# Loading weight blocks from ScalarE's DMA queue, each behind an exponential, in a fused attention and feed-forward kernel

## The chip, the cores and the metric

The kernel runs on one core of one Trainium2 chip. The metric is the device time of one execution in microseconds. Engines are named as in the profile: PE is TensorE (matmuls; PEld its weight loads), DVE is VectorE, ACT is ScalarE, POOL is GpSimd, and SP is SyncE, which issues DMAs. A row "SPq" is SP's DMA queue.

## The reference

Masked attention over 8 batches of 8 heads with 576 rows and a head size of 64, and behind it a feed-forward layer of 512 to 2048 to 512 with softplus on all 4608 tokens:

```python
scores = scale * np.matmul(q, k.transpose(0, 1, 3, 2))
thresh = np.max(scores, axis=-1, keepdims=True) - tau
scores = np.where(scores >= thresh, scores, -1000000000.0)
scores = scores - np.max(scores, axis=-1, keepdims=True)
attn = np.exp(scores)
attn = attn / (np.sum(attn, axis=-1, keepdims=True) + 1e-09)
attn_out = np.matmul(attn, v).astype(np.float32)
x = attn_out.transpose(0, 2, 1, 3).reshape(B * S, H * D)
h = x @ w_in
g = np.maximum(h, 0.0) + np.log1p(np.exp(-np.abs(h)))
return (g @ w_out).astype(np.float32)
```

q, k, v and tau are float32. The weights w_in (512 x 2048) and w_out (2048 x 512) arrive as 64-bit floats, so the kernel has to make 32-bit ones of them.

## The kernel before

**Attention.** The work is 32 units, a batch and a pair of heads each, and each unit has 9 query tiles of 128 rows: 288 tiles. A tile goes through a fixed chain: scores on PE (L423, tile `s`), the row maximum and the threshold on DVE (`negm`, `thr`, L430 and L431), the exponential on ACT (`exps`, L435, into one half of `e_all`), the mask by threshold and the row sum on DVE (`mask`, L440, in place in `e_all`), the transpose of the weights on PE (L471, L474, tiles `tm` and `tr`), and a copy of them by ACT (`gH`, L498 to L519). `e_all` and `s` have two halves, so two tiles are in flight at a time. ACT also casts the transposed keys (`kT`, L368 and L390) and queries (`qT`, `qm`, L377 and L396) for PE.

**Feed-forward.** The 4608 tokens are 9 chunks of 512. Their matmuls (`h` L645 to L649, `o` L703 to L707) are mixed between the attention tiles, from the moment the weights are there.

**Weights.** They come in 32 blocks of 512 KB. i0_0 to i3_3 are blocks of w_in (128 rows by 512 columns), o0 to o15 of w_out; about one new block starts every two tiles. The function `to_f32` takes one block through these steps:

- a DMA of the 64-bit words into `words` (the profile's `wc_i` or `wc_o`; L185),
- `first`, set down `WD = 4` points (two tiles) later: ACT's Abs of the high words, scaled, into `wa_i` or `wa_o` (L193), and POOL's clamp (L194),
- `second`, three steps on DVE (L200, L202, L205), each put behind the latest emitted mask by an order dependency (`behind`, with the list `masked`),
- `parts`, two steps on POOL that split the block into a high and a low part (L125, L132),
- for w_in, two stores on SP to a scratch tensor in HBM (`wi_d`, L234), from which the feed-forward stage loads it again.

All DMAs are on SP's queue: the words of the weights, the loads of k, q and v (`kn`, `qn`, `vn`, L306 to L321), the swaps of halves of the queries (L385, L386), the stores of the weights' parts and of the attention's output (`x_d`, L597), the feed-forward's loads. SP executes them in order, so a load stands behind whatever waits ahead of it.

`took` is the number of weight-sized buffers that a block finds free for its words and its scratch. It is 2 for 29 of the 32 blocks; for o12, o14 and o15 it is less.

**What sets the order.** The program emits the instructions in a planned sequence, and a scheduler of the framework then orders each engine's instructions by its own model of durations, within the dependencies. `tc.add_manual_dep(..., NoSync, ...)`, called by `behind`, adds a dependency that holds on the same engine's order without a semaphore. A semaphore that tells that a DMA has landed is one of eight, taken in turn over all DMAs; a DMA waits until the one that used its semaphore before has landed.

Of the kernel before, what the change touches and what calls it, by code (L numbers as in the profile page):

```python
# [11 lines left out]
U32 = mybir.dt.uint32  # L12
AF = mybir.ActivationFunctionType
# [46 lines left out]
def tile_kernel(ctx: ExitStack, tc: tile.TileContext, q, k, v, tau, w_in, w_out, out):  # L60
# [8 lines left out]
    nc = tc.nc  # L69
# [5 lines left out]
    HS = S // 2  # L75
# [47 lines left out]
    def hi_of(eng, out_, in_):  # L123
        if eng is nc.gpsimd:
            eng.tensor_scalar(out=out_, in0=in_, scalar1=1.0, scalar2=1.0, op0=ALU.mult, op1=ALU.mult)  # L125
        elif eng is nc.scalar:
            eng.copy(out_, in_)  # L127
        else:
            eng.tensor_copy(out_, in_)  # L129

    def lo_of(eng, out_, in_, hi):
        eng.tensor_tensor(out=out_, in0=in_, in1=hi.bitcast(F32), op=ALU.subtract)  # L132
# [3 lines left out]
    free, held = [NFC], [0]  # L136

    masked = []
    scored = []

    def behind(i, others):

        if others:
            tc.add_manual_dep(i.ins, others[-1].ins.name, mybir.DependencyInfo(
                mybir.DependencyClass.NoSync, mybir.DependencyReason.DATA), reason="order")

    def piece(dt, name):
        return cpool.tile([P, 2, DM], dt, tag="wo", bufs=NFC, name=name)

    def to_f32(src, want, name, then):  # L150

        keep = 1 if want else 0
        while free[0] < 1 + keep and free[0] < NFC - held[0]:
            force()
        took = max(0, min(2, free[0] - keep))
        if took:
            words = piece(F32R, f"wc_{name}")
        else:  # L160
            words = wpool.tile([P, 2, DM], F32R, tag="wi", bufs=WB, name=f"wc_{name}")
        if took > 1:
            m = piece(F32, f"wa_{name}")[:, 0, :]
        else:
            m = fpool.tile([P, 512], F32, tag="st", bufs=NST, name=f"ws_{name}")
        free[0] -= took + keep
        held[0] += keep

        later_ = defer if took > 1 else lambda n, f: f()
        step = 2 if held[0] < NFC // 2 else 1  # L170
        w = piece(F32R, f"wo_{name}") if want else words

        def done():
            free[0] += took

        def parts():
            hi_of(nc.gpsimd, w[:, 0, :], m)
            lo_of(nc.gpsimd, w[:, 1, :], m, w[:, 0, :])

        if src.dtype == F32:  # L180
            nc.sync.dma_start(m, src)
            later_(WD, lambda: then(parts, w, done))
            return
        words = words.bitcast(U32).rearrange("p a n -> p (a n)")
        nc.sync.dma_start(words, src.bitcast(U32))  # L185
        words = words.rearrange("p (n t) -> p n t", t=2)
        low, high = words[:, :, 0], words[:, :, 1]
        mu = m.bitcast(U32)

        def first():
            nc.scalar.activation(m, high.bitcast(F32), AF.Abs, scale=2.0 ** 16)  # L193
            nc.gpsimd.tensor_scalar(out=m, in0=m, scalar1=W_MAX, scalar2=W_MIN, op0=ALU.min, op1=ALU.max)  # L194
            later_(1, lambda: second(0))


        def second(n):
            if n == 0:
                i = nc.vector.tensor_scalar(out=mu, in0=mu, scalar1=3, scalar2=None, op0=ALU.logical_shift_left)  # L200
            elif n == 1:
                i = nc.vector.scalar_tensor_tensor(out=mu, in0=high, scalar=0x80000000, in1=mu,  # L202
                                                   op0=ALU.bitwise_and, op1=ALU.bitwise_or)
            else:
                i = nc.vector.scalar_tensor_tensor(out=mu, in0=low, scalar=29, in1=mu,  # L205
                                                   op0=ALU.logical_shift_right, op1=ALU.bitwise_or)
            if took > 1:
                behind(i, masked)
            if n < 2:
                later_(step, lambda: second(n + 1))  # L210
            else:
                later_(1, lambda: then(parts, w, done))

        later_(WD, first)
# [12 lines left out]
    def prep_w_in(g, cc):  # L227
        def split(parts, w, free):
            parts()
            defer(WS, lambda: store(w.bitcast(F32), free))  # L230

        def store(w, free):
            for i in range(2):
                nc.sync.dma_start(wi_d[g][:, :, i, cc, :].rearrange("f p e -> p f e"),  # L234
                                  w[:, i, :].rearrange("p (f e) -> p f e", f=4))
            free()
            if cc == NCC - 1:
                ready.add(("i", g))

        to_f32(w_in[cc * P:(cc + 1) * P, g * 512:(g + 1) * 512], False, f"i{g}_{cc}", split)  # L240

    def prep_w_out(fc):
        def split(parts, w, free):
            wo[fc] = w
            parts()
            free()
            ready.add(("o", fc))

        to_f32(w_out[fc * P:(fc + 1) * P, :], True, f"o{fc}", split)
# [25 lines left out]
    for b in range(B):  # L275
        for kind in (("one", "two") if b < NSPLIT else ("all",)):
            for hp in range(NPAIR):
                s = Unit()
# [123 lines left out]
    e_all = cpool.tile([P, 2, S], F32, name="e_all")  # L402
# [29 lines left out]
        s.m[t] = (negm, thr)  # L432

    def exps(s, t):
        nc.scalar.activation(e_all[:, s.half[t], :].rearrange("p (h n) -> p h n", h=2), s.sp[t][:, :, 0:HS],  # L435
                             AF.Exp, bias=s.m[t][0], scale=1.0)

    def mask(s, t):
        e2 = e_all[:, s.half[t], :].rearrange("p (h n) -> p h n", h=2)
# [362 lines left out]
    def force():  # L802
        _, f = later.pop(0)
        f()
# [32 lines left out]
    for kind, g in WL:  # L837
        for m in range(4):
            n = len(prep)
# [75 lines left out]
    scores(*tiles[0])  # L915
    row_max(*tiles[0])
    exps(*tiles[0])
    scores(*tiles[1])
    for j in range(2):
# [4 lines left out]
    for g, (cur, t) in enumerate(tiles):  # L924
# [5 lines left out]
        for step in PAT0 + ("m" if g == TG - 1 else "") if g < TG else PAT:  # L930
            if step == "T":
                weights_T(cur, t)
            elif step == "h":
                weights_hi(cur, t)
            elif step == "l":
                weights_lo(cur, t)
            elif step == "R" and nxt:
                row_max(*nxt)
            elif step == "e" and nxt:
                exps(*nxt)  # L940
            elif step == "m" and nxt:
                mask(*nxt)
            elif step == "M":
                mask(cur, t)
            elif step == "f":
                upto += quota / PAT.count("f")
                while done < upto:
                    done += next(ffn)
            elif step == "x":
                extras(cur.i, cur.tiles.index(t))  # L950
            elif step == "S" and g + 2 < NS:
                scores(*tiles[g + 2])
            elif step == "v":
                slow_products()
            elif step == "w":
                while prep and prep[0][0] <= g:
                    _, f, a = prep.pop(0)
                    f(*a)
            elif step == "p":
                point()  # L960
# [38 lines left out]
```

## Time and profile before

| | |
|---|---|
| runs of before | 1448.56, 1449.85, 1451.9 us; median 1449.85 |
| profiled execution | 1451.43 us, span 1449.6 us |
| mean granted clock of PE | 0.996 |
| PE busy | 1398.8 us, 96% of the span |
| DVE, ACT, POOL busy | 987.2, 847.1, 590.3 us |
| weight loads on SP | 16 of w_in, first issue at 13.5 us, last at 181.6; 16 of w_out, 54.9 to 256.8 |

A row of the timeline gives the start in us from the span's start, the duration in us, the engine, the line, the operation, the output and the input by the program's names with their numbers left out, the shapes, and in brackets the idle time of the engine ahead of it and what ended that. A row of waits gives the engine and line that waited, what it waited for, the total in us, how many times, and the longest. A row of windows gives the stretch, its length, busy time of PE, PEld, DVE, ACT and POOL with instruction counts, the granted clock of PE (1.00 is full), the share of time that the DMA engines were busy, and GB/s.

### The profile page before, as it was taken

The page shows a single profiled execution, that of the slowest core. Times are in us where ns is not written, and L with a number is a line of the kernel's source. Part 1 is how long each engine was busy: PE and PEld are TensorE (multiplying, and loading weights), DVE is VectorE, ACT ScalarE, POOL GpSimd, SP SyncE. Part 2 cuts the span into 40 slices and gives each one's busy share as a digit, 9 for nine tenths or more (in the row PEclk, how much of TensorE's full clock was granted, in tenths as well). Part 3 has the DMA queues.
Part 4 walks back from the last instruction along what each step waited for, and adds up shares of the span by engine and source line. Part 5 has one row for each costly group of instructions (what it writes and reads, how often), then busy time and mean ns, then how long its engine had stood idle before and what let it go on. Part 6 is the DMA issues. An engine that isn't in the chain of part 4 may idle for free.

```text
span 1449.6 us, 23487 instructions
## 1 busy us (share of the span) xinstructions
PE 1398.8 (96%) x7860; PEld 1161.8 (80%) x7860; DVE 987.2 (68%) x2211; ACT 847.1 (58%) x1615; POOL 590.3 (41%) x619
## 2 busy tenths in 40 slices
PE   6887999999999999999999999999999999999998
PEld 4555688788888888888888888888888888788886
DVE  6988588787777777777777777777777777402111
ACT  6667667667656576657665665667665765311010
POOL 3667566443333333344334333344334431324221
PEclk9999999999999999999999999999999999999999
DMA  5866765445333533445433533354344432333321
GB/s 170 227 186 206 214 191 182 126 121 160 104 106 114 135 109 116 119 132 151 122 111 96 154 105 100 117 151 120 113 119 135 147 99 73 105 126 130 118 86 44
DMA packets 131208, 189.93 MB, mean 131 GB/s; under 512 B 35312, under 2 KB 86800, under 8 KB 131088
## 3 DMA queue, kind: packets, MB, share of 16 engines
q1 hardware_dynamic: 131088, 188.43, 44.5%
q8 instruction: 63, 1.03, 0.3%
q14 instruction: 57, 0.47, 0.1%
HBM read 140.51 MB, written 27.41 MB: 116 GB/s over the span
## 4 chain that ended last, share of the span: by engine, by line
PE 78%; DVE 8%; ACT 4%; issue 3%; DMA 3%; POOL 3%; SPq 1%; POOLq 0%; DVEq 0%; ACTq 0%
PE s L423 10%; PE h L647 9%; PE h L645 9%; PE h L649 8%; PE o L707 8%; PE o L705 8%; PE o L703 8%; PE s L474 7%; PE pv L555 3%; PE pv L556 3%; PE tr L364 2%; DVE e_all L440 2%; DVE negm L430 2%; POOL g L132 1%; DMA wc_i<-in_moe_w_in_dram 1%
## 5 line engine op out<-in xcount | busy, mean ns | idle before, releaser
L132 POOL TENSOR_TENSOR g<-st,g 128x512 fp32r<-128x512 f32 x144 | 191.6, 1348 | 195.6 <-DVE g L129 184.2
L440 DVE SCALAR_TENSOR_TENSOR e_all<-s,thr,e_all 128x576 f32<-128x576 f32 x288 | 234.6, 816 | 49.1 <-ACT e_all L435 45.8
L430 DVE TENSOR_REDUCE negm<-s 128x1 f32<-128x576 f32 x288 | 217.2, 754 | 43.5 <-PE s L423 36.0
L707 PE MATMUL o<-wo_o,g 128*128 128x512 f32 x576 | 232.5, 404 | 5.3 <-POOL g L132 5.3
L435 ACT ACTIVATE e_all<-s,negm 128x576 f32<-128x576 f32 x288 | 216.0, 750 | 33.5 <-PE tr L471 14.8
L647 PE MATMUL h<-xl,wi 128*128 128x512 f32 x576 | 233.9, 406 | 0.9 <-POOL xl L132 0.9
L703 PE MATMUL o<-wo_o,g 128*128 128x512 f32 x576 | 232.3, 403 | 0.8 <-DVE acc L720 0.4
L645 PE MATMUL h<-xh,wi 128*128 128x512 f32 x576 | 230.6, 400 | 2.3 <-ACT xh L127 2.0
L649 PE MATMUL h<-xh,wi 128*128 128x512 f32 x576 | 230.6, 400 | 0.0
L705 PE MATMUL o<-wo_o,g 128*128 128x512 f32 x576 | 228.4, 397 | 0.0
L498 ACT CAST gH<-s 128x512 fp32r<-128x512 f32 (+1 forms) x270 | 145.1, 550 | 140.6 <-PE s L474 137.8
L132 DVE TENSOR_TENSOR gL<-s,gH 128x512 fp32r<-128x512 f32 (+1 forms) x270 | 169.0, 634 | 46.4 <-ACT gH L498 24.0
L423 PE MATMUL s<-kT,qT 128*128 128x288 f32 x1024 | 193.1, 310 | 7.6 <-ACT gH L512 2.0
L423 PEld LDWEIGHTS s<-kT,qT 128*128 128x128 f32 x1024 | 149.3, 191 | 28.2 <-issue 10.8
L129 DVE CAST g<-st 128x512 fp32r<-128x512 f32 x128 | 57.4, 485 | 149.5 <-ACT st L667 149.0
L474 PE MATMUL s<-identr,e_all 128*128 128x128 f32 x1008 | 154.6, 276 | 3.9 <-DVE e_all L440 3.9
L667 ACT ACTIVATE st<-h 128x512 f32<-128x512 f32 x144 | 78.3, 596 | 115.6 <-PE h L649 115.0
L707 PEld LDWEIGHTS o<-wo_o,g 128*128 128x128 f32 x576 | 108.4, 188 | 29.2 <-POOL g L132 11.0
L474 PEld LDWEIGHTS s<-identr,e_all 128*128 128x128 f32 x1008 | 114.8, 141 | 20.7 <-DVE e_all L440 12.5
L645 PEld LDWEIGHTS h<-xh,wi 128*128 128x128 f32 x576 | 108.9, 189 | 26.1 <-ACT xh L127 2.6
L647 PEld LDWEIGHTS h<-xl,wi 128*128 128x128 f32 x576 | 108.9, 189 | 23.2 <-POOL xl L132 1.7
L649 PEld LDWEIGHTS h<-xh,wi 128*128 128x128 f32 x576 | 109.0, 189 | 21.9
(107 smaller groups left out, 2363.4 us busy)
## 6 DMA issues: line engine op xcount, KB each, us to landing
wi<-wi_d SPq DMA_DIRECT2D x144, 512.0 KB
qT<-qT SPq DMA_DIRECT2D x124, 128.0 KB
R<-r_d SPq DMA_DIRECT2D x64, 144.0 KB
kn<-in_k_dram SPq DMA_DIRECT2D x32, 256.0 KB
qn<-in_q_dram SPq DMA_DIRECT2D x32, 256.0 KB
vn<-in_v_dram SPq DMA_DIRECT2D x32, 256.0 KB
wc_i<-in_moe_w_in_dram SPq DMA_DIRECT2D x16, 512.0 KB
wi_d<-wc_i SPq DMA_DIRECT2D x32, 256.0 KB
```

The source lines that it names most:

```text
L132: eng.tensor_tensor(out=out_, in0=in_, in1=hi.bitcast(F32), op=ALU.subtract)
L423: i = nc.tensor.matmul(sp[:, hf, 0:HS], lhs, s.kT[j][:, k0 + hf * HS:k0 + (hf + 1) * HS], start=(m == 0), stop=(m == len(parts) - 1))
L430: nc.vector.reduce_max(negm, s.sp[t][:, :, 0:HS], axis=AX.XY, negate=True)
L435: nc.scalar.activation(e_all[:, s.half[t], :].rearrange("p (h n) -> p h n", h=2), s.sp[t][:, :, 0:HS], AF.Exp, bias=s.m[t][0], scale=1.0)
L440: masked.append(nc.vector.scalar_tensor_tensor(out=e2, in0=s.sp[t][:, :, 0:HS], scalar=s.m.pop(t)[1], in1=e2, op0=ALU.is_ge, op1=ALU.mult, ...
L474: nc.tensor.matmul(main[:, c, :], e[:, c0:c0 + P], ident, is_transpose=True, start=True, stop=True)
L645: nc.tensor.matmul(h, wi[:, 0, cc, :], u.h[cc], start=(cc == 0), stop=False)
L647: nc.tensor.matmul(h, wi[:, 0, cc, :], u.l[cc], start=False, stop=False)
L649: nc.tensor.matmul(h, wi[:, 1, cc, :], u.h[cc], start=False, stop=(cc == NCC - 1))
L703: nc.tensor.matmul(o, gh[:, sl], wo[fc][:, 0, :], start=(i == 0), stop=False)
L705: nc.tensor.matmul(o, gh[:, sl], wo[fc][:, 1, :], start=False, stop=False)
L707: nc.tensor.matmul(o, gl[:, sl], wo[fc][:, 0, :], start=False, stop=(i == QF - 1))
```

## The change

A list `powers` collects the exponentials as they are emitted. A weight block whose `took` is above 1 (29 of 32) is loaded by a DMA that ACT issues, with an order dependency behind the latest exponential emitted so far. The other three stay on SP. The rest of the code is as it was, five lines further down from there on.

```diff
     masked = []
+    powers = []
     scored = []
 ...
-        nc.sync.dma_start(words, src.bitcast(U32))
+
+        if took > 1:
+            behind(nc.scalar.dma_start(words, src.bitcast(U32)), powers)
+        else:
+            nc.sync.dma_start(words, src.bitcast(U32))
         words = words.rearrange("p (n t) -> p n t", t=2)
 ...
     def exps(s, t):
-        nc.scalar.activation(e_all[:, s.half[t], :].rearrange("p (h n) -> p h n", h=2), s.sp[t][:, :, 0:HS],
-                             AF.Exp, bias=s.m[t][0], scale=1.0)
+        powers.append(nc.scalar.activation(e_all[:, s.half[t], :].rearrange("p (h n) -> p h n", h=2), s.sp[t][:, :, 0:HS],
+                             AF.Exp, bias=s.m[t][0], scale=1.0))
```

The scheduler then orders all engines anew up to about unit 8; behind that the orders are the same. In the rows below the third number of a weight block's name is the program's running number: `wc_i_1_307`, `wc_i_2_381`, `wc_i_3_457`, `wc_i_0_535` are blocks i0_1, i0_2, i0_3, i1_0. ACT before, around tiles 5 to 7 of the first unit, with no issue among its rows and the Abs of i0_3 behind tile 5's copy:

```order
L514 COPY gH_2_363<-tr_4_351 64x64
L390 CAST kT_0_339<-tr_0_2_371 128x2x64
L396 ACTIVATE qm<-tr_0_2_371,qscale 128x64 x2
L377 ACTIVATE qT_1_0_379<-tr_0_1_374,qscale 128x512
L435 ACTIVATE e_all<-s_142,negm_6_394 128x576
L498 COPY gH_2_363<-tm_5_399 128x4x128
L193 ACTIVATE wa_i_3_458<-wc_i_3_457 128x512
L435 ACTIVATE e_all<-s_143,negm_7_420 128x576
```

and ACT in the changed kernel at the same place:

```order
L519 COPY gH_2_363<-tr_4_351 64x64
L188 DMA wc_i_2_381<-in_moe_w_in_dram 128x1024
L395 CAST kT_0_339<-tr_0_2_371 128x2x64
L401 ACTIVATE qm<-tr_0_2_371,qscale 128x64 x2
L382 ACTIVATE qT_1_0_379<-tr_0_1_374,qscale 128x512
L440 ACTIVATE e_all<-s_142,negm_6_394 128x576
L503 COPY gH_2_363<-tm_5_399 128x4x128
L198 ACTIVATE wa_i_2_382<-wc_i_2_381 128x512
L440 ACTIVATE e_all<-s_143,negm_7_420 128x576
```

The load of i0_2 is now issued there, and its Abs, which stood ahead of the exponential of tile 4 before, stands one exponential behind its issue, where the Abs of the next block stood.

DVE before, from the maximum of tile 7 to its mask (L200, L202 and L205 are the three steps of a weight block):

```order
L430 TENSOR_REDUCE negm_7_420<-s_143 128x1
L440 SCALAR_TENSOR_TENSOR e_all,sums_218<-s_142,thr_6_395,e_all 128x576
L431 TENSOR_SCALAR thr_7_421<-negm_7_420,ntau 128x1
L205 SCALAR_TENSOR_TENSOR wa_i_1_308<-wc_i_1_307,wa_i_1_308 128x512
L200 TENSOR_SCALAR wa_i_2_382<-wa_i_2_382 128x512
L440 SCALAR_TENSOR_TENSOR e_all,sums_218<-s_143,thr_7_421,e_all 128x576
L430 TENSOR_REDUCE negm_8_469<-s_142 128x1
```

and in the changed kernel:

```order
L445 SCALAR_TENSOR_TENSOR e_all,sums_218<-s_142,thr_6_395,e_all 128x576
L210 SCALAR_TENSOR_TENSOR wa_i_1_308<-wc_i_1_307,wa_i_1_308 128x512
L205 TENSOR_SCALAR wa_i_2_382<-wa_i_2_382 128x512
L445 SCALAR_TENSOR_TENSOR e_all,sums_218<-s_143,thr_7_421,e_all 128x576
L435 TENSOR_REDUCE negm_8_469<-s_142 128x1
```

The steps of i0_2 keep their place ahead of tile 7's mask, though its Abs on ACT has moved back by two tiles.

SP before, around the first stores of weight parts:

```order
L185 DMA wc_i_3_457<-in_moe_w_in_dram 128x1024
L234 DMA wi_d_90<-wc_i_0_253 128x4x128 x2
L385 DMA qm<-qm 64x256
L386 DMA qm<-qm 64x256
L385 DMA qT_1_0_380<-qT_1_0_379 64x512
L386 DMA qT_1_0_380<-qT_1_0_379 64x512
L185 DMA wc_i_0_535<-in_moe_w_in_dram 128x1024
L234 DMA wi_d_90<-wc_i_1_307 128x4x128 x2
```

and in the changed kernel:

```order
L326 DMA vn_529<-in_v_dram 64x2x64 x2
L239 DMA wi_d_90<-wc_i_0_253 128x4x128 x2
L314 DMA kn_865<-in_k_dram 128x2x256
L311 DMA kn_865<-in_k_dram 64x64
L390 DMA qm<-qm 64x256
L391 DMA qm<-qm 64x256
L390 DMA qT_1_0_380<-qT_1_0_379 64x512
L391 DMA qT_1_0_380<-qT_1_0_379 64x512
L311 DMA kn_865<-in_k_dram 64x64
L239 DMA wi_d_90<-wc_i_1_307 128x4x128 x2
```

The weight loads are gone from SP, and a load of k that stood behind the third pair of stores now stands behind the first.

## Prediction

> **What bounds the kernel now.** I read the page's busy line and its chain first, to see which engine sets the end, and then a table of windows, to see where that engine is not full, since only there can a moved load cost or save anything.
>
> ```profile
> span 1449.6 us, 23487 instructions
> PE 1398.8 (96%) x7860; PEld 1161.8 (80%) x7860; DVE 987.2 (68%) x2211; ACT 847.1 (58%) x1615; POOL 590.3 (41%) x619
> PE 78%; DVE 8%; ACT 4%; issue 3%; DMA 3%; POOL 3%; SPq 1%; POOLq 0%; DVEq 0%; ACTq 0%
> ```
>
> TensorE is busy for 1398.8 of 1449.6 us. The chain leaves it for VectorE, ScalarE, DMA and POOL in 19% of the span, so there is a stage where others set the pace. The windows show which:
>
> ```profile
> 20.00:40.00 20.00, 17.54 (x108) 12.30 (x107) 16.96 (x40) 15.43 (x35) 10.13 (x13) 1.00 0.68 201
> 40.00:60.00 20.00, 17.24 (x103) 11.73 (x102) 17.82 (x38) 14.96 (x37) 14.91 (x18) 1.00 0.80 236
> 100.00:120.00 20.00, 14.89 (x94) 10.59 (x92) 15.61 (x33) 12.71 (x31) 13.54 (x18) 1.00 0.61 180
> 180.00:200.00 20.00, 20.00 (x117) 16.51 (x116) 16.04 (x33) 15.66 (x32) 12.98 (x14) 1.00 0.73 214
> 200.00:300.00 100.00, 97.54 (x567) 80.42 (x567) 84.79 (x190) 67.07 (x126) 56.41 (x63) 1.00 0.50 148
> ```
>
> The columns are length, busy PE, PEld, DVE, ACT, POOL, granted clock and DMA share. PE lacks 2.46 us of 20 in the first row and 5.11 in the third, and nothing at 180:200. PE's work is fixed, so before about 180 us every microsecond in which the attention tiles stand still is a microsecond of the end. After it, a late weight block has PE's queue of FFN matmuls in front of it. The weights come in from 13 to 257 us:
>
> ```profile
> L185 SPq DMA_DIRECT2D wc_i<-in_moe_w_in_dram x16: 347/544/1070, 13.5 to 181.6; - x16
> L185 SPq DMA_DIRECT2D wc_o<-in_moe_w_out_dram x16: 334/512/666, 54.9 to 256.8; - x16
> ```
>
> (ns least/median/most of one issue on SP, and the us at which the first and the last start.) The waits of 0 to 270 us that touch the weights:
>
> ```profile
> POOL wa_i L194 <- ACT wa_i L193: 21.6, 10, 4.8
> ACT wa_i L193 <- DMA wc_i<-in_moe_w_in_dram: 12.5, 7, 3.9
> DVE wa_i L200 <- POOL wa_i L194: 7.5, 5, 3.1
> ACT wa_o L193 <- DMA wc_o<-in_moe_w_out_dram: 3.7, 5, 1.3
> SPq L234 <- POOL wc_i L125: 20.4, 8, 6.7
> ```
>
> ScalarE stands 16.2 us behind loads that have not landed. SP stands 20.4 us behind POOL's split for the scratch stores, with later loads queued behind them. These are what the change could give back.
>
> **The change part by part.**
>
> *What it removes: loads late because of SP.* The places where it hurts now, and where TensorE then has a gap:
>
> ```profile
> 18.07 0.67 ACT L193 ACTIVATE wa_i<-wc_i 128x512 f32<-128x512 f32 x1 [3.89 <-DMA wc_i<-in_moe_w_in_dram]
> 21.88 0.66 PE L474 MATMUL tm<-identr,e_all 128*128 128x128 f32 x4 [1.58 <-DVE e_all L440]
> 48.70 0.67 ACT L193 ACTIVATE wa_i<-wc_i 128x512 f32<-128x512 f32 x1 [1.47 <-DMA wc_i<-in_moe_w_in_dram]
> 49.27 0.72 ACT L435 ACTIVATE e_all<-s,negm 128x576 f32<-128x576 f32 x1
> 105.92 0.43 DVE L200 TENSOR_SCALAR wa_i<-wa_i 128x512 uint32<-128x512 uint32 x1 [1.83 <-POOL wa_i L194]
> 108.97 0.67 ACT L193 ACTIVATE wa_i<-wc_i 128x512 f32<-128x512 f32 x1 [3.35 <-DMA wc_i<-in_moe_w_in_dram]
> ```
>
> I take 1.0 of the 3.89 (most of it lies beside other waits of the first tiles), 1.3 of PE's 1.58 at 21.88, all 1.47 at 48.70 (the next exponential starts right behind it, at 49.27), 0.9 of VectorE's 1.83, and 1.2 of the 3.35, since the load there is again issued late in the new order. That is −5.9. The ends are 0 and about −12, the sum of the same five waits taken whole.
>
> *What it adds: short leads.* Now a load is issued on SP and read by ScalarE's Abs two tiles later. In the new order ScalarE issues it behind an exponential and reads it after one or two. For block i0_2 the issue stands where before's `CAST kT` is (29.23), and its Abs where before's Abs of i0_3 is (31.45). A load needs longer than that, from issue to Abs, where ScalarE waits for it:
>
> ```profile
> 29.23 0.29 ACT L390 CAST kT<-tr 128x128 fp32r<-128x128 f32 x1
> 31.45 0.72 ACT L193 ACTIVATE wa_i<-wc_i 128x512 f32<-128x512 f32 x1
> 33.25 0.74 ACT L435 ACTIVATE e_all<-s,negm 128x576 f32<-128x576 f32 x1 [1.08 <-PE tr L471]
> 33.73 0.58 SPq L185 DMA_DIRECT2D wc_i<-in_moe_w_in_dram  x1
> 34.03 0.82 DVE L440 SCALAR_TENSOR_TENSOR e_all<-s,thr,e_all 128x576 f32<-128x576 f32 x1
> 38.38 0.68 ACT L193 ACTIVATE wa_i<-wc_i 128x512 f32<-128x512 f32 x1 [0.75 <-DMA wc_i<-in_moe_w_in_dram]
> 43.51 0.58 SPq L185 DMA_DIRECT2D wc_i<-in_moe_w_in_dram  x1
> ```
>
> 33.73 to 38.38 is 4.65 us, and 43.51 to 48.70 is 5.19. So i0_2 lands at 29.23 + 4.65 = 33.9, its Abs ends at 34.55, and the exponential of tile 7, queued behind it, starts at 34.5 instead of 33.25. On VectorE the block's first step stands ahead of that tile's mask. It can start only after POOL's clamp:
>
> ```profile
> 32.41 0.61 POOL L194 TENSOR_SCALAR wa_i<-wa_i 128x512 f32<-128x512 f32 x1
> 33.48 0.41 DVE L200 TENSOR_SCALAR wa_i<-wa_i 128x512 uint32<-128x512 uint32 x1
> ```
>
> 34.55 + 0.61 = 35.2, plus 0.4 for the step: the mask starts at 35.6, not 34.03, so 1.6 us of the tile chain. Block i1_0's issue stands in the same way at the first of these two rows, and its Abs at the second, 2.17 us later:
>
> ```profile
> 41.13 0.28 ACT L390 CAST kT<-tr 128x128 fp32r<-128x128 f32 x1
> 43.30 0.69 ACT L193 ACTIVATE wa_i<-wc_i 128x512 f32<-128x512 f32 x1
> ```
>
> The same reading by before's start times gives nine blocks leads of 1.8 to 2.7 us (i0_2, i0_3, i1_0, o3, i2_0, i2_1, i2_2, o10, o13) against loads that take 4.05 to 5.19. i2_2 is in the sum above, o10 and o13 come when PE is full. The other six I estimate at 1.6, 0.9, 1.9, 1.5, 1.0 and 1.6 us: together +8.5. The lower end is +2: the slack of 1.08 at 33.25 stands ahead of other exponentials too, and each delay shifts the next one's issue and lets the next load hide. The upper end is +13, six times a shortfall of 4.65 − 2.4.
>
> *What it adds: ScalarE's issues.* 29 issues leave SP for ScalarE; 19 of them before 180 us. On SP one takes 0.544 us (w_in); no row shows one on ScalarE. The nearest rows are SP's own, so I take 0.55: 10.5 us of ScalarE's time in the stage. It is busy for 15.43 of 20 us there, and on the chain for a small part, so I let a quarter through: +2.6. Ends: 0 (ScalarE has 4 to 7 us of idle in each 20) and all 10.5.
>
> *What it moves on SP.* SP loses 29 × 0.54 = 15.7 us of issues, and its loads of k, q and FFN input come up to a few rows earlier. It is not the bound: its own waits (20.4 us above) are for POOL. Each completion semaphore is shared by every eighth load or store, so a ScalarE issue can also wait until an SP transfer of the same semaphore has landed; k's load ahead of i0_3 is one. One such wait may cost ScalarE 1 to 2 us. I set the two against each other: 0, ends −2 and +3.
>
> The Trainium skill, DMA: Bandwidth & Descriptors, section "Issuing engines are not separate DMA queues", says that DMAs started on different engines run on the same 16 DMA engines, and that issuing from several saves only sequencer time. This trace's DMA share of 0.80 at 40:60 neither proves nor refutes it; by that rule the landing times would stay as they are, which is what the rows of the sum assume, and the gain would be no more than SP's issue time.
>
> *Sum:* −5.9 + 8.5 + 2.6 + 0 = +5.2 us. The profiled execution took 1451.43 us, 1.58 more than the median of the runs, 1449.85. So 1456.6 against its own time and 1455 against the median. 0.2%, 2.9 us, is about what a measurement of this kernel can tell from no change.
>
> **The rivals.**
>
> *Faster (0.29).* The waits go and the short leads hardly bite. For it: once ScalarE runs a little later everywhere, the lead grows by as much; some loads took only 4.05 us (54.89 to 58.94). Against it: the loads that ScalarE waits for now had 4.5 to 5.2 us and still came late. With the short leads at +2 and the issues at +1.5, −5.9 + 3.5 = −2.4; should one half-clock stretch vanish as well, 1.7 more:
>
> ```profile
> 54.89 0.46 SPq L185 DMA_DIRECT2D wc_o<-in_moe_w_out_dram  x1
> 58.94 0.67 ACT L193 ACTIVATE wa_o<-wc_o 128x512 f32<-128x512 f32 x1 [0.99 <-DMA wc_o<-in_moe_w_out_dram]
> 86.00:88.00 2.00, 2.00 (x5) 0.85 (x5) 1.82 (x5) 0.68 (x2) 1.92 (x3) 0.50 0.63 148
> 154.00:160.00 6.00, 5.64 (x15) 4.58 (x16) 1.25 (x3) 2.15 (x5) 2.77 (x4) 0.50 0.73 212
> ```
>
> That is −4.1: about 1445.7. It decides once the six short leads cost less than 0.55 us each on the mean (−5.9 + 2.6 + 6 × 0.55 = 0).
>
> *No change (0.17).* PE's idle in this stage has several causes at once: where a load no longer holds the exponential, the mask of VectorE does. With gains and losses each about 4 the time stays within 1447 to 1452.7.
>
> *Much slower (0.12).* Each ScalarE wait holds exponentials, copies of the transposed weights and casts for TensorE; two or three more gaps of TensorE near 2 us bring stretches at half clock. The window rows show 0.50 in 86:88 and in 154:160; a stretch of some 3.4 us (estimated from the neighbouring windows) at half costs 1.7. With the short leads at +13 and issues at +5, and two such stretches, −5.9 + 18 + 3.4 = +15.5: 1465.
>
> The Trainium skill, TensorE: Matmul & The Clock Gate, section "Part 1", says that the gate closes when TensorE has not been busy enough lately; the 0.50 rows agree, and no run here shows yet whether the change moves such a stretch.
>
> **How the numbers follow.** My forecast, slower by 3 to 11 us, has 0.42; the others stand above. Faster 0.29, same 0.17, slower 0.42 + 0.12 = 0.54. The range leaves out about one in ten on each side: 1442 (below the faster rival's 1445.7, where gains come nearer to their end of −12) to 1467 (above the much slower case). The forecast's own range is 1452.8 to 1461.
>
> **What would show each step.** Removed waits: ScalarE's wait for w_in loads at the places 18.07, 21.99 and 48.70 is gone, and SP's row for L185 holds three issues. Short leads: ScalarE's total wait for the w_in and w_out loads is not below 16.2 but about 18, in pieces of about 2 us, most between 30 and 125 us, with VectorE's first step waiting for POOL longer than 7.5 us. Issues: rows of ACT's queue of about 0.5 us each. PE's busy time in 20:60 falls below 34.78 of 40; from 200 us on nothing changes but a shift. I am wrong if landing from ScalarE takes 3 us or less, if the issues delay ScalarE by the full 0.55 each, or if a half-clock stretch comes or goes and outweighs the rest.

## The result, and the profile after

The changed kernel takes 1474.35 us (median of 4 runs, 1470.73 to 1477.44), against 1449.25 before (4 runs): ratio 1.0164, 95% interval 1.0142 to 1.0186. It is slower by some 24 us; 5 were forecast. The page of the changed kernel, its busy line and chain, the 180 us in which the pace is set (first row: before, second: after; columns as in the windows above), and the loads' issues:

```profile
span 1472.2 us, 23475 instructions
PE 1404.8 (95%) x7860; PEld 1165.7 (79%) x7860; DVE 979.2 (67%) x2211; ACT 850.0 (58%) x1615; POOL 589.1 (40%) x619
PE 79%; DVE 7%; ACT 4%; DMA 4%; POOL 3%; issue 3%; SPq 0%; ACTq 0%; POOLq 0%; DVEq 0%
```

```profile
0.00:180.00 180.00, 147.45 (x796) 102.16 (x797) 137.42 (x285) 120.52 (x263) 108.07 (x131) 0.97 0.69 199
```

```profile
0.00:180.00 180.00, 132.64 (x694) 91.15 (x695) 119.98 (x260) 105.67 (x235) 95.18 (x120) 0.92 0.63 180
...
L188 ACTq DMA_DIRECT2D wc_i<-in_moe_w_in_dram x16: 334/334/380, 13.7 to 200.5; - x16
```

The span grew by 22.6 us. 6.0 of them are PE's busy time (1398.8 to 1404.8: the same 7860 matmuls at a lower clock, 0.92 against 0.97 in the first 180 us). 16.6 are idle time of PE, 14.8 of it before 180 us (147.45 − 132.64). The place was as forecast, the size and the way were not. The waits for the weights and for R in the first 270 us, after:

```profile
POOL xp L598 <- DMA R<-r_d: 15.3, 5, 5.2
DVE wa_i L205 <- POOL wa_i L199: 13.4, 7, 6.1
ACT wa_i L198 <- DMA wc_i<-in_moe_w_in_dram: 6.8, 6, 1.9
DVE wa_o L205 <- POOL wa_o L199: 4.2, 3, 2.6
ACT wa_o L198 <- DMA wc_o<-in_moe_w_out_dram: 0.6, 2, 0.4
```

ScalarE's wait for the loads fell from 16.2 to 7.4 us, so the change does what it says. But POOL now waits 15.3 us for R (the row scales that come back over HBM; no such row was in before's list), and VectorE 17.6 us for POOL's clamp, where it was 7.5 + 2.3. SP's loads of k, q and v wait for POOL's split of k (total, times, longest; before, then after):

```profile
SPq L309 <- POOL k L132: 11.0, 2, 5.7
```

```profile
SPq L314 <- POOL k L132: 29.3, 6, 8.4
```

The first two large gaps of PE that the kernel before does not have show what happened. The first is at 41 us. Before, SP started unit 1's swaps at 31.19:

```profile
31.19 0.50 SPq L385 DMA_DIRECT2D qm<-qm  x1
```

After (rows of SP, then PE):

```profile
33.10 0.37 SPq L314 DMA_DIRECT2D kn<-in_k_dram  x1
33.53 0.65 SPq L311 DMA_DIRECT2D kn<-in_k_dram  x1
34.28 0.54 SPq L390 DMA_DIRECT2D qm<-qm  x1
...
36.15 0.59 SPq L391 DMA_DIRECT2D qT<-qT  x1
...
41.47 0.85 PE L428 MATMUL s<-kT,qT 128*128 128x288 f32 x2 [2.94 <-DMA qT<-qT]
```

k's load for unit 3, which the new order puts ahead of unit 1's swaps, waited 1.2 us for POOL to free its buffer. The swaps started at 34.28 instead of 31.19, and PE stood 2.94 us for them. The second is at 74 us (rows of SP, POOL, DVE and PE):

```profile
58.24 0.37 SPq L634 DMA_DIRECT2D wi<-wi_d  x1
58.65 1.11 SPq L592 DMA_DIRECT2D R<-r_d  x2
...
66.94 1.41 POOL L598 TENSOR_TENSOR xp<-xp,R 128x576 f32<-128x576 f32 x1 [5.22 <-DMA R<-r_d]
...
71.05 0.61 POOL L199 TENSOR_SCALAR wa_i<-wa_i 128x512 f32<-128x512 f32 x1
...
71.70 0.43 DVE L205 TENSOR_SCALAR wa_i<-wa_i 128x512 uint32<-128x512 uint32 x1 [6.07 <-POOL wa_i L199]
...
74.43 0.61 PE L428 MATMUL s<-kT,qT 128*128 128x288 f32 x1 [4.81 <-DVE e_all L445]
```

A feed-forward load of 512 KB, which stood behind unit 3's R before, now stands between unit 0's store of its row scales and its load of R. POOL waits for R, its clamp of a weight block stands behind that, VectorE's first step of the block waits for the clamp, the mask behind that step waits too, and PE stands 4.81 us. By the starts of the exponentials the loss builds up over the first four units: unit 1's first tile is 6.0 us late (45.48 against 39.51), unit 2's 12.8 (79.70 against 66.89), unit 3's 17.7 and unit 4's 21.4.

### The profile page after: what moved, and what is told of

The parts are those of the page before. It is cut to its first block, busy times and chain, and to the rows that moved or that the text cites. A ratio compares the mean times of both kernels' runs of the same rounds, so it can differ in the third digit from the quotient of the medians.

```text
span 1472.2 us, 23475 instructions
## 1 busy us (share of the span) xinstructions
PE 1404.8 (95%) x7860; PEld 1165.7 (79%) x7860; DVE 979.2 (67%) x2211; ACT 850.0 (58%) x1615; POOL 589.1 (40%) x619
## 4 chain that ended last, share of the span: by engine, by line
PE 79%; DVE 7%; ACT 4%; DMA 4%; POOL 3%; issue 3%; SPq 0%; ACTq 0%; POOLq 0%; DVEq 0%
PE s L428 11%; PE h L652 9%; PE h L650 9%; PE h L654 8%; PE o L712 8%; PE o L710 7%; PE o L708 7%; PE s L479 7%; PE pv L560 3%; PE pv L561 3%; PE tr L369 2%; DVE negm L435 2%; DVE e_all L445 2%; PE pv L554 1%; POOL g L132 1%
## 5 line engine op out<-in xcount | busy, mean ns | idle before, releaser
L712 PEld LDWEIGHTS o<-wo_o,g 128*128 128x128 f32 x576 | 108.4, 188 | 29.2 <-POOL g L132 11.0
L650 PEld LDWEIGHTS h<-xh,wi 128*128 128x128 f32 x576 | 108.8, 189 | 27.2 <-ACT xh L127 3.5
L708 PEld LDWEIGHTS o<-wo_o,g 128*128 128x128 f32 x576 | 108.5, 188 | 23.4 <-DVE g L129 2.1
```

Source lines behind the costliest of these rows:

```text
L650: nc.tensor.matmul(h, wi[:, 0, cc, :], u.h[cc], start=(cc == 0), stop=False)
L708: nc.tensor.matmul(o, gh[:, sl], wo[fc][:, 0, :], start=(i == 0), stop=False)
L712: nc.tensor.matmul(o, gl[:, sl], wo[fc][:, 0, :], start=False, stop=(i == QF - 1))
```

## The experiments

Most of them pin the order of engines. The program's instructions carry the same numbers in both kernels, so a table of numbers per engine can set the order with the same kind of dependency that `behind` uses:

```diff
+    for seq in ORDER:
+        names, at_ = [], 0
+        for d in seq.split():
+            at_ += int(d)
+            names.append(f"I-{at_}")
+        for a, b in zip(names, names[1:]):
+            tc.add_manual_dep(nc.get_inst_by_name(b), a, mybir.DependencyInfo(
+                mybir.DependencyClass.NoSync, mybir.DependencyReason.DATA), reason="order")
```

Ratios below are to the kernel before on the same chip.

**Control: the changed kernel pinned to its own orders.**

> Control: the changed kernel with all its orders pinned to its own. 1470 to 1478 in any theory; otherwise pinning itself changes the time, and all comparisons of pinned kernels with the changed one are off by that.

1472.59 us, ratio 1.0153 (1.0138 to 1.0168): pinning changes nothing that can be told.

**Only the issue moved.** The loads go to ScalarE, PE, DVE, ACT, POOL and SP keep the order of before. One thing could not be kept: on ScalarE a load stands behind the Abs of the block before, which is emitted ahead of it. So some loads stand later than on SP. (Lines with `ORDER` and rows of names, here and below, stand for the tables of numbers.)

```diff
-            behind(nc.scalar.dma_start(words, src.bitcast(U32)), powers)
+            nc.scalar.dma_start(words, src.bitcast(U32))
 # ORDER: SP as before without the 29 loads; ACT as before with the loads in it; DVE, POOL, PE as before
```

> The 29 loads are issued by ScalarE, but every engine's order is pinned to that of the kernel before: SP's without the loads, ScalarE's with each load at the place of its old issue time, though not ahead of the Abs of the block before it (leads of 2.1 to 14 us by before's times). Theory A (the loss of 24 us comes from the new order of SP's queue, where loads of k, q, v and of the feed-forward stand ahead of swaps and of R): 1447 to 1453. Theory B (short leads and the issues on ScalarE themselves cost it): 1455 to 1475. Theory C (the new order on PE, DVE, ACT and POOL costs it): 1447 to 1453.

1456.77 us, ratio 1.0035 (1.0021 to 1.0050). That is a fifth of what the change costs. Of the ranges written down only theory B's holds it, near its lower end; A and C had expected no loss here. It is also the size that I had forecast for the whole change, but by chance: ScalarE still waits 13.5 us for loads here, so most of the waits are still there, and its Abs come 3.9 us or more behind their loads' issues, so the leads are not short.

**The same with SP's new order.**

```diff
 # ORDER of SP, here around unit 0's R
 r_d_109<-rt_604
+wi_0_1733<-wi_d_90
 R_607<-r_d_109 x2
```

> As the issue-only kernel, but SP's queue in the order of the changed kernel; PE, DVE, ACT and POOL in the order of before. Theory A: 1465 to 1475, most of the 24 us are back. Theory B and theory C: within 3 us of the issue-only kernel.

1469.15 us, ratio 1.0131 (1.0110 to 1.0152): 14 us of the loss come with SP's order alone (0.0096 of 1450). The rows of SP and POOL with the loads on ScalarE and SP in its old order, then in its new one:

```profile
51.89 0.35 SPq L588 DMA_DIRECT2D r_d<-rt  x1
53.96 1.10 SPq L592 DMA_DIRECT2D R<-r_d  x2
...
59.84 1.41 POOL L598 TENSOR_TENSOR xp<-xp,R 128x576 f32<-128x576 f32 x1
```

```profile
54.94 0.54 SPq L588 DMA_DIRECT2D r_d<-rt  x1
...
58.58 0.37 SPq L634 DMA_DIRECT2D wi<-wi_d  x1
58.99 1.38 SPq L592 DMA_DIRECT2D R<-r_d  x2
...
66.72 1.40 POOL L598 TENSOR_TENSOR xp<-xp,R 128x576 f32<-128x576 f32 x1 [6.25 <-DMA R<-r_d]
```

R was issued 2.07 us behind the store of the scales, now 4.05: the feed-forward load ahead of it waited 2.3 us for a scratch store (`wi_d`) to land. R is POOL's longest wait in this stretch, and the first tile of unit 2 then starts 7.9 us later (78.94 against 71.01). The changed kernel comes to the same place (79.70) by the same wait, but there R is issued 2.1 us behind the store and only lands late.

**SP's old order in the changed kernel, the rest left to the scheduler.**

> The changed kernel with SP's queue pinned to the order of before (without the 29 loads); the scheduler orders the other engines. Theory A: 1447 to 1457. Theory B: 1466 to 1476. Theory C: 1462 to 1476, unless the scheduler orders the other engines otherwise once SP's order is given.

1464.57 us, ratio 1.0093 (1.0073 to 1.0113). Some 10 us come back, not 20. That is in the range of theory C alone, but the scheduler has drawn the other engines' order anew here, so it decides little. It speaks against A as the whole. B's range is missed by 1.4 us, which alone is too little to rule B out; the kernel with SP's new order does that for most of the loss, since 14 us came there while ScalarE's order stayed as it was.

**The loads back on SP, all orders of the changed kernel.**

```diff
-            behind(nc.scalar.dma_start(words, src.bitcast(U32)), powers)
+            nc.sync.dma_start(words, src.bitcast(U32))
 # ORDER: PE, DVE, ACT, POOL, SP as in the changed kernel, the loads at the same times on SP
```

> All engines in the order of the changed kernel, but the 29 loads are issued by SP again, each ahead of the first SP row that started after ScalarE's issue of it in the changed kernel's trace: the same leads and the same order, without issues on ScalarE. Theory A and theory C: 1470 to 1477. Theory B, the part of it that is ScalarE's issues: 1463 to 1470; its short leads stay as they are.

1473.8 us, ratio 1.0156 (1.0137 to 1.0176). With the changed kernel's orders it makes no difference which engine issues.

**The feed-forward's first loads moved away from R.** All orders of the changed kernel, but its first three `wi` loads stand on SP behind unit 3's R, or in a second kernel behind unit 2's:

```diff
 r_d_109<-rt_604
-wi_0_1733<-wi_d_90
 R_607<-r_d_109 x2
```

> All orders of the changed kernel, but on SP the first three loads of the feed-forward's weights (wi of the first chunk) stand behind unit 3's load of R, as they do in the kernel before, and no longer between the first unit's store of r_d and its load of R. Theory A1 (these loads make R late, POOL waits for R with the clamp behind it, DVE for the clamp with the masks behind it): 1464 to 1470, 5 to 9 us less than the changed kernel, with tile 0 of unit 2 at least 5 us earlier. Theory A2 (the loads of k, q and v ahead of swaps and R are what costs): within 2 us of 1474. Theory C (the other engines' order): within 3 us of 1474.

> All orders of the changed kernel, but on SP the first three loads of the feed-forward's weights stand behind unit 2's load of R: out of the way of unit 0's and unit 1's R, yet early enough for the first feed-forward matmul, which waited 3.14 us for them where they stood behind unit 3's. Theory A1 (they delay R, and what is won there stays won unless they come late themselves): 1465 to 1470. If what SP's order takes at one place is always given back at another: 1472 to 1476.

1474.65 us (ratio 1.0156, 1.0135 to 1.0177) and 1472.88 (1.0141, 1.0117 to 1.0164). Where it was made, the gain is there: with the loads behind unit 3's R, unit 0's R is issued at 59.03, no earlier than in the changed kernel (58.65), and is at hand 3 us earlier (63.87 against 66.94):

```profile
63.87 1.54 POOL L598 TENSOR_TENSOR xp<-xp,R 128x576 f32<-128x576 f32 x1 [1.28 <-DMA R<-r_d]
```

POOL's waits for R fall from 15.3 to 7.0 us. Tile 0 of unit 2 starts 3.4 us earlier (76.31 against 79.70), less than the 5 I had asked for, and tile 8 at 104.97 instead of 110.59. Unit 4 starts 8.6 us earlier (138.55 against 147.11), and at its end the gain is gone (unit 5 at 192.06 against 191.82). In the first kernel PE stands there twice, once for a mask and once, in a feed-forward matmul, for the moved load:

```profile
145.47 1.12 PE L479 MATMUL s<-identr,e_all 128*128 128x128 f32 x4 [4.71 <-DVE e_all L445]
163.61 0.50 PE L650 MATMUL h<-xh,wi 128*128 128x512 f32 x1 [3.14 <-DMA wi<-wi_d]
```

The first of these gaps is in the second kernel too, at 148.19. In both the same chain runs over another load, v's, with POOL's clamp behind it (rows of the second kernel: POOL, DVE, PE):

```profile
143.41 0.46 POOL L125 TENSOR_SCALAR vt<-vn 128x320 fp32r<-128x320 f32 x1 [3.98 <-DMA vn<-in_v_dram]
143.95 0.61 POOL L199 TENSOR_SCALAR wa_o<-wa_o 128x512 f32<-128x512 f32 x1
...
144.59 1.07 DVE L205 TENSOR_SCALAR wa_o<-wa_o 128x512 uint32<-128x512 uint32 x1 [4.42 <-POOL wa_o L199]
...
148.19 0.89 PE L479 MATMUL s<-identr,e_all 128*128 128x128 f32 x4 [4.34 <-DVE e_all L445]
```

**More rows of SP put back.** In addition k's load for unit 3 goes behind unit 1's swaps, and v's, q's and x loads behind the R that they stood ahead of, with `wi` behind unit 3's R or unit 2's.

> As the one with the feed-forward's loads moved, and besides on SP: k's load for unit 3 behind the swaps of unit 1's queries, v's loads for units 3 and 4, q's for unit 6 and the first x load of the feed-forward each behind the load of R that they stood ahead of. Theory A (all of SP's order): 1458 to 1464. Theory A1 (only the feed-forward's loads): as the kernel with those alone. Theory C: 1468 or more.

> As that, and k's load for unit 3 behind the swaps of unit 1, v's for units 3 and 4, q's for unit 6 and the first x load behind the R they stood ahead of. Theory A (SP's order carries half or more of the loss): 1458 to 1464. If the order of the other engines carries most of it: 1468 to 1475.

1468.29 us (1.0122, 1.0098 to 1.0147) and 1466.91 (1.0115, 1.0090 to 1.0139): 4 to 7 us of the 24 (by the control or by the changed kernel itself), and hardly clear of noise: the first's interval overlaps both of theirs, the second's touches the control's. Both are short of theory A's range, so by the medians these rows of SP do not carry half of the loss.

The two places named above are mended by it, though. In the first kernel's profile the first tile of unit 1 starts at 40.47 (45.48 in the changed kernel) and that of unit 2 where the issue-only kernel has it (71.01), not where the changed kernel has it (79.70):

```profile
71.53 0.74 ACT L440 ACTIVATE e_all<-s,negm 128x576 f32<-128x576 f32 x1 [2.83 <-PE tr L476]
```

This profile is of the fastest of four executions, which lie 10 us apart (1462.88 to 1472.89); so it shows what the rows do at these places, not what they are worth at the end.

**The fourth corner: SP's old order under the new order of the other engines.**

> The fourth corner: PE, DVE, ACT and POOL in the order of the changed kernel, SP in the order of before without the 29 loads, except three x loads of the feed-forward, which stand where the changed kernel needs them (behind unit 1's R and behind the swaps of units 3 and 4). If the parts add up (issue 5, SP's order 13, the others' order 5): 1458 to 1463. If the other engines' order carries as much when SP's is undone (the two orders act through the same waits): 1464 to 1470.

1498.42 us, ratio 1.0340 (1.0315 to 1.0364). Neither range holds it: it is the slowest of all. (Three loads of `x` could not go back, as the expectation says.) POOL and SP wait for each other's order there:

```profile
POOL q L125 <- DMA qn<-in_q_dram: 25.5, 2, 18.3
```

```profile
SPq L239 <- POOL wc_i L125: 46.4, 13, 12.5
```

So SP's order has no price of its own, and the 14 us above hold under the old orders of the other engines. It costs by how it fits the orders of the engines that free its buffers and wait for its loads.

**Without the exponential in front.** The changed kernel with the dependency left out:

> The changed kernel without the order dependency on an exponential: loads on ScalarE's queue wherever the scheduler puts them. If the exponential in front is what makes the order bad: 1450 to 1460. If moving the loads off SP, and with it the scheduler's new order, does it (theories A and C): 1465 to 1480.

1464.73 us, ratio 1.0094 (1.0074 to 1.0113): slower than before by 14 us, 10 us less than with it, again on an order of the scheduler's own. That lies between the two ranges, so the exponential in front is neither the whole cause nor shown to be harmless.

**Two loads on their way.** WD = 6: the Abs comes a tile later, behind the next block's load. The second kernel is the one before with the same edit, as a control.

```diff
-WD = 4
+WD = 6
```

> The changed kernel with WD = 6 in place of 4: Abs of a block is emitted a tile later, behind the next block's load, so two loads can be on their way. Theory B (one load in flight at a time, short leads): 1455 to 1464. Theory A or C (order of SP and of the other engines, which the scheduler draws up anew here too): 1465 to 1478.

> Control for WD = 6: the kernel before with WD = 6, all loads on SP. If later Abs in itself is what helps or hurts: as far from before as the changed kernel with WD = 6 is from the changed kernel. If not: 1447 to 1455.

1485.04 us, ratio 1.0239 (1.0221 to 1.0257); the control 1.0013 (1.0004 to 1.0023). In the changed kernel with WD = 6 ScalarE's waits for loads are down to one of 1.5 us, and it is 11 us slower than the changed kernel, above both ranges. VectorE's wait for the clamp of the w_in blocks has doubled (13.4 us in the changed kernel):

```profile
DVE wa_i L205 <- POOL wa_i L199: 28.2, 13, 5.7
...
ACT ws_o L198 <- DMA wc_o<-in_moe_w_out_dram: 1.5, 1, 1.5
```

**One link of the chain moved.** VectorE's weight steps one mask later; or POOL's multiplication with R behind the next clamp. All else as in the changed kernel.

> All orders of the changed kernel, but on VectorE each of the three steps of a weight block stands behind one more mask. Theory D (POOL's clamp comes late, for R or for ScalarE, and VectorE's first step waits for it with masks queued behind: 17.6 us in the changed kernel): 1460 to 1468, and VectorE's wait for the clamp below 8 us. Theory A (SP's order acts on the tiles through R, swaps and v in other ways): 1470 to 1477.

> All orders of the changed kernel, but on POOL the multiplication with R stands behind the next clamp, for five units, so POOL no longer waits for R with that clamp queued behind. Theory A1' (R's lateness acts only through the clamp behind it on POOL): 1464 to 1469. Theory D with other causes of the late clamp: 1470 to 1475.

1482.2 us (1.0218, 1.0199 to 1.0237) and 1483.76 (1.0231, 1.0209 to 1.0253): both slower, both against my expectation. With POOL's multiplication later its wait for R is 2.4 us and VectorE's for the clamp 7.6, but SP's store of the scaled values waits for it, and the swaps stand behind that store:

```profile
PE s L428 <- DMA qT<-qT: 19.5, 5, 5.3
```

With VectorE's steps later POOL waits for them (`wc_i` 42.0 us in 11 waits, 12.2 in the changed kernel), and VectorE's own wait for POOL hardly falls (16.4 us from 17.6). So this kernel does not show what the changed one would take without that wait.

**What the removed waits are worth.** The kernel before with its own orders and SP issuing all, but each of the first 20 loads stands where the load before it stood. In a second kernel the first of them goes ahead of v's load for unit 1 as well.

```diff
 qn_188<-in_q_dram x3
+wc_i_0_253<-in_moe_w_in_dram
 vn_232<-in_v_dram
 qm<-qm x2
 vn_232<-in_v_dram x2
-wc_i_0_253<-in_moe_w_in_dram
+wc_i_1_307<-in_moe_w_in_dram
 kn_521<-in_k_dram x3
-wc_i_1_307<-in_moe_w_in_dram
+wc_i_2_381<-in_moe_w_in_dram
```

> The kernel before, all orders pinned to its own, but each of the first 20 weight loads stands on SP at the place where the load before it stood (the first directly ahead of that): loads a block earlier, everything on SP. If ScalarE's waits for loads (16.2 us before) cost the tile chain 3 to 6 us, as my sum had it: 1444 to 1448. If they lie beside other waits: 1449 to 1453. If k, q and v behind the loads get too late: over 1453.

> The kernel before with its own orders, the first 20 weight loads a block earlier on SP, and the first of them besides ahead of v's load for unit 1. ScalarE's last long wait for a load (3.66 us at 17.95 in the kernel with loads a block earlier) goes: 1445 to 1448, if it lies on the path; 1448 to 1450 if VectorE's masks hold the first tiles anyway.

1448.83 us (ratio 0.9985, 0.9975 to 0.9995) and 1448.44 (0.9983, 0.9972 to 0.9993). Both are faster than before by some 2 us, less than the 3 to 6 expected, and so faster than both the kernel before and the changed one. In the second the waits for the loads are nearly gone:

```profile
ACT wa_o L193 <- DMA wc_o<-in_moe_w_out_dram: 3.1, 3, 1.8
...
ACT wa_i L193 <- DMA wc_i<-in_moe_w_in_dram: 1.3, 2, 1.0
```

and at the first of them another wait stands in its place:

```profile
14.98 0.66 ACT L193 ACTIVATE wa_i<-wc_i 128x512 f32<-128x512 f32 x1 [0.34 <-DMA wc_i<-in_moe_w_in_dram]
17.80 0.58 ACT L498 COPY gH<-tm 128x512 f32<-128x512 f32 x1 [2.16 <-PE tm L474]
```

**The first four loads left on SP**, the other 25 on ScalarE, all orders of before:

> The issue-only kernel (all orders of before), with the first four loads issued by SP at their old places and 25 by ScalarE. Theory: the 5.5 us of the issue-only kernel come from loads that on ScalarE can't stand ahead of the Abs of the block before, most of it (3.2 us) at the first tiles: 1451 to 1455. If ScalarE's issues cost it evenly: 1455 to 1457.

1454.43 us, ratio 1.0027 (1.0014 to 1.0040), against 1.0035 (1.0021 to 1.0050) with all 29 on ScalarE. The median is in the theory's range, but the intervals overlap, so the times do not show where those 5 us lie. The profiles, one execution each, speak for the theory in part: at the last tile of unit 2 the issue-only kernel is 3.8 us behind the kernel before (96.00 against 92.23), this one 0.9 (93.10). Both lose more behind unit 3.

## Why the prediction was wrong

**The sign, and where.** Slower was right, and so was the stretch before 180 us with PE's gaps and the lower clock. But most of the loss came by a path that the sum had put at 0, and its two largest terms were both too high, so that the sign came out right is in good part luck. The time is 24 us over before where the sum gave 5.2, and outside the range.

**"What it moves on SP": this is the step that failed.** It took the shared semaphores against earlier loads and came to 0, with ends −2 and +3. With the other engines in their old order, SP's new order alone took the ratio from 1.0035 to 1.0131, 14 us. The rows were there to be read: k's load ahead of the swaps is in the order shown with the change. I priced it as a load that comes earlier. It is a row that waits for POOL, with swaps behind it for which PE waits. The prediction gave SP's waits by one row, 20.4 us for the scratch stores; the same list has 11.0 us of loads behind POOL's split of k, and these became 29.3. Nor did it look at what else had moved up: the feed-forward's loads ahead of R were not even quoted. The semaphores, which it did price, show little on SP: apart from the waits of R and `x` for their own data, its longest wait for a DMA in the first 270 us is 1.1 us.

**What the sum had no term for: the order of PE, DVE, ACT and POOL.** The sum followed only the weights' steps through it. From 1.0131 to 1.0164 the intervals overlap, so it may be some 5 us, or less. The fourth corner shows that the terms do not add: undoing SP's order alone costs 26 us more (1498.42 against the control's 1472.59).

**"Removed waits", −5.9.** The waits went, as forecast. Their price was too high: with 16.5 us of waits (12.5, 3.7 and a 0.3 at the last blocks) brought down to 5.2 (1.3, 3.1 and 0.8) and no other engine's order changed, the gain is 0.17%, about 2.5 us. The sum counted as gain what another wait lay behind, as the 2.16 us for PE at 17.80 shows.

**"Short leads", +8.5, and "about 18 us in pieces of about 2".** ScalarE waited 7.4 us, the longest piece 1.9. Before 180 us no Abs came less than 3.3 us behind its load's issue, and i0_2's, for which the sum had 2.2, came 4.3 behind. The leads grew as the tiles slowed, which the faster rival had said. That they were not what cost most is shown by SP's order: 14 us came with ScalarE's order unchanged. WD = 6 fits this (almost no wait for loads, and 1485 us), though all orders are new there.

**"ScalarE's issues", +2.6.** One took 0.334 us, not 0.55, and with the orders held, taking them back to SP won nothing that can be told (1.0156 against 1.0164 and 1.0153). What is left of the issue-only kernel's 5 us is not settled. In its profile the first tiles lose 3.2 us, where a load could not stand ahead of the Abs of the block before; with the first four loads left on SP the profile loses about half of that there, but the time is not clear of noise from the issue-only kernel's.

**The Trainium skill's rule** (DMA: Bandwidth & Descriptors, "Issuing engines are not separate DMA queues"), that another issuing engine saves sequencer time and no more, holds here: same orders, other engine, same time (1.0156 against 1.0164 and 1.0153).

**The much slower rival** came nearest in size, 1465, and had the lower clock (PE's busy time is up 6.0 us for the same matmuls), but the wrong chain: loads that hold ScalarE. What held, as the rows around 74 us show it, was SP, POOL and VectorE in a ring: a transfer late on SP holds POOL, POOL's clamp holds VectorE's masks, those hold PE, and the late tile's stores hold SP's swaps. A wait taken out at one link came back at the next in four kernels (the first `wi` loads moved in two ways, WD = 6, and POOL's multiplication moved).

What stays open is which rows of the new orders carry the loss. Putting back the rows of SP that I could name mended unit 1's and unit 2's start, and won 4 to 7 us of 24 by the medians.

## What to carry to other kernels

Where a scheduler orders the engines, moving one queue's transfers is a change to every engine's order. Read the new order of the queue that got lighter first: look for each row that moved up, whether it waits for something, and who waits for the rows now behind it. To learn what an edit itself is worth, pin all orders to the old ones; here that parted 5 us from 24. The sum of an engine's waits is no bound to reckon a gain from: 11 us of waits taken away gave 2.5.

## What the runs showed of the hardware that I had not expected

A DMA issue took 0.334 us on ScalarE's queue (median of 16, 0.334 to 0.380), against a median of 0.544 on SP's for the same loads. That is not shown to be a price of the engine: of the 32 weight loads that SP issues in the kernel before, the three that start more than 0.2 us after SP's last issue took 0.334, 0.334 and 0.347, and the 29 that follow more closely took 0.364 to 1.070. One of the three:

```profile
21.99 0.35 SPq L185 DMA_DIRECT2D wc_i<-in_moe_w_in_dram  x1
```

An issue on ScalarE lies beside the engine's own work: the issue at 63.49 stands within the copy that starts at the same time and takes 0.59 us.

```profile
63.49 0.59 ACT L503 COPY gH<-tm 128x512 f32<-128x512 f32 x1 [0.28 <-PE tm L479]
63.49 0.33 ACTq L188 DMA_DIRECT2D wc_i<-in_moe_w_in_dram  x1
63.97 0.67 ACT L198 ACTIVATE wa_i<-wc_i 128x512 f32<-128x512 f32 x1
```

The load of R (two of 144 KB, unit 0's) lands later with a 512 KB load issued just ahead of it. From the end of its last issue to POOL's row that waits for it are 7.2 us in the changed kernel (59.76 to 66.94) and 5.7 in the pinned control (61.43 to 67.12), where the feed-forward load starts 0.4 us ahead; 3.7 (60.14 to 63.87) and 3.5 (61.50 to 64.99) in the two kernels that differ from the control in these loads alone. Without the exponential in front, where the feed-forward load starts 2.2 us ahead of R, it was 2.9 (65.71 to 68.57). These are single executions.
